# Dealing the MLP units of a decode kernel to partitions in runs of 4, with b1 loaded as rows

## The chip, the cores and the metric

The kernel runs on one core of one Trainium2 chip. The time is device microseconds (us) of one execution, lower is better. A median is over the runs of one kernel. A trace is one profiled execution; its times count from the start of the span.

## The reference, cut to what matters

```python
h  = x + attention(layernorm(x), k_cache, v_cache, wq, wo)   # 4 x 32 heads x 4096 keys x 128, bf16
hn = layernorm(h)                                            # 4 rows of 640
u  = hn @ w1 + b1                                            # w1: 640 x 1728
a  = u * tanh(softplus(u))                                   # mish
h2 = h + a @ w2                                              # w2: 1728 x 640
```

The caches are 268 MB and are read once. The MLP is small, but it comes last. Its 1728 hidden units may be dealt to the 128 partitions in any order, as long as the columns of w1, the elements of b1 and the rows of w2 are dealt alike.

## The kernel before: the parts that matter

Five engine programs run side by side. One queue (issued by SP) loads in this order: wq, all K and V tiles, wo, w1 in three pieces (2, 2 and 1 of the 5 row groups), w2 in four. The small loads go through ACT's queue. 1728 = 13 * 128 + 64, so there are 13 full groups of 128 units and a rest of 64.

```python
W1S = (0, 2, DC - 1, DC)          # pieces of w1
W2S = (0, 6, 10, 12, FM)          # pieces of w2: 6+4+2+1 of 13 row groups (FM = 13)

# b1: partition p holds units 13p .. 13p+12, runs of 26 B; the rest of 64 units 2 B each
load(ac, b1T[:, 0:FM], B_b1[0 : FM * P].rearrange("(p j) -> p j", j=FM), "b1a", "S")
load(ac, b1T[0:FT, FM : FM + 1], B_b1[FM * P : F].rearrange("(p o) -> p o", o=1), "b1b", "S")

# w2: the same dealing, 13 rows running for each partition
w2_v = B_w2[0 : FM * P, :].rearrange("(p j) n -> p j n", j=FM)
for k, (j0, j1) in enumerate(zip(W2S, W2S[1:])):
    load(sp, w2_sb[:, j0:j1, :], w2_v[:, j0:j1, :], ("w2", j0), ...)

# TensorE: w1 is the stationary operand; group j is every 13th column
for c0, c1 in zip(W1S, W1S[1:]):
    # ... before the last piece: two matmuls add b1_hi and b1_lo ...
    pe.need(("w1", c0))
    for j in [FM] + list(range(FM)):
        for c in range(c0, c1):
            if j < FM:
                w = w1_sb[:, c, 0 : FM * P].rearrange("p (f j) -> p j f", j=FM)[:, j, :]
            else:
                w = w1_sb[:, c, FM * P : F]
            mm(h1_ps[...], w, cen[:, c, :], ...)
# ... then DVE and ACT: h1, exp, mish -> act; TensorE: 4 matmuls for each row group of w2 ...
for j0, j1 in zip(W2S, W2S[1:]):
    pe.need(("w2", j0))
    for j in range(j0, j1):
        w2_mm(j)
```

The softmax here doesn't subtract the row's maximum and nothing guards it: scores larger than these inputs give would overflow.

## Time and profile before

| | before |
|---|---|
| median of 3 runs | 662.52 us (662.31 to 663.42) |
| span of the profiled run | 661.0 us |
| read from HBM | 283.35 MB, 429 GB/s over the span |
| busy: DVE, PE | 62%, 58% |

The page of the kernel before has one row of the DMA engines' busy tenths, in 40 slices of 16.5 us, and the page gives the rate over the span:

```profile
DMA  9999999999999999999999999999999999999997
HBM read 283.35 MB, written 0.01 MB: 429 GB/s over the span
```

DMA is the limit of everything but the end: only the last slice is below nine tenths. What comes behind the last landings is a chain of compute. In order of time, the last pieces of the chain of waits of the kernel before (start us, length us, what):

```profile
628.31 23.43 DMA slotB<-in_B_w_dram
651.73 0.04 issue
651.78 3.07 PE red L714 x44
...
654.87 0.23 DVE h L677
...
656.42 0.23 DVE act L703
656.64 0.04 issue
656.69 2.16 PE red L714 x55
658.85 0.02 issue
658.87 0.33 DVE o_bf L710
```

The second piece of w1 lands at 651.73 us. From there to o_bf at 658.87 us nothing but compute is on the chain. The timeline of the same stretch gives the groups (start us, length us, engine, line, operation, output and inputs, count, and in brackets the idle time before with what ended it; PEld is the weight load):

```profile
651.78 1.83 PEld L714 LDWEIGHTS red<-cen,slotB 128*64 128x64 bf16 x28 [0.21 <-DMA slotB<-in_B_w_dram]
653.74 1.01 PEld L714 LDWEIGHTS red<-cen,slotB 128*64 128x64 bf16 x14
656.69 0.30 PE L714 MATMUL red<-w_tail,act 64*4 64x160 bf16 x4 [1.10 <-DVE act L703]
656.92 1.90 PE L714 MATMUL red<-slotA,act 128*4 128x160 bf16 x52
```

The w1 loads take 1.83 us for 28 and 1.01 us for 14; in steady state one starts every 58 to 61 ns. (A row of the timeline is named by the shape of its first load; of the 28, two have 64 columns and 26 have 128.) The 52 w2 matmuls run in 1.90 us, 36.5 ns each on average, without a wait. The pieces of w2 land at 655.08, 656.67, 657.45 and 657.84 us by the trace, so each has landed when it is reached, but the last less than 1 us ahead.

### The profile page before, as it was taken

What the parts mean: (1) busy time and instruction counts of PE and PEld (TensorE: products, weight loads), DVE (VectorE), ACT (ScalarE), POOL (GpSimd) and SP (SyncE); (2) the same over time, 40 slices, a digit from 0 to 9 for tenths busy, and PEclk for the clock granted to TensorE, in tenths of its full rate; (3) what the DMA queues carried; (4) which work ended last, traced back from release to release, by engine and by line L of the source; (5) the groups of instructions that cost most, each with busy time, mean ns of one, the idle gap of its engine ahead of it and who ended that gap; (6) DMA issues with size and microseconds to landing.
All of it is one profiled execution on the core that took longest, in us unless ns stands there. A gap on an engine that the chain in (4) does not pass through costs nothing. (4 is left out here: it accounts for less than half of the span.)

```text
span 661.0 us, 4948 instructions
## 1 busy us (share of the span) xinstructions
PE 386.6 (58%) x2623; PEld 70.5 (11%) x1663; DVE 407.4 (62%) x255; ACT 40.7 (6%) x157; POOL 1.7 (0%) x12
## 2 busy tenths in 40 slices
PE   0356667457317595838307485828534757675877
PEld 0100010101101010101100010100110001010146
DVE  2067889386049778677219688948306798857612
ACT  0200000000000000000000000000000000000011
POOL 0000000000000000000000000000000000000000
PEclk9998698879659796869668778977965879786865
DMA  9999999999999999999999999999999999999997
GB/s 386 444 440 444 421 408 445 437 441 437 429 420 440 436 436 436 440 428 424 444 432 432 440 428 424 444 432 433 444 436 432 424 440 428 440 440 428 412 418 303
DMA packets 7121, 283.48 MB, mean 429 GB/s; under 512 B 1028, under 2 KB 1352, under 8 KB 2376
## 3 DMA queue, kind: packets, MB, share of 16 engines
q1 hardware_dynamic: 6784, 283.27, 99.2%
q10 hardware_dynamic: 328, 0.09, 0.1%
q8 instruction: 6, 0.10, 0.1%
q14 instruction: 3, 0.02, 0.0%
HBM read 283.35 MB, written 0.01 MB: 429 GB/s over the span
## 5 line engine op out<-in xcount | busy, mean ns | idle before, releaser
L513 DVE TENSOR_TENSOR slotA<-slotA,q_bc 128x8192 bf16<-128x8192 bf16 x32 | 140.6, 4415 | 106.2 <-DMA slotA<-in_A_k_cache_dram 106.2
L513 DVE TENSOR_TENSOR slotB<-slotB,q_bc 128x8192 bf16<-128x8192 bf16 x32 | 140.7, 4416 | 17.6 <-DMA slotB<-in_A_k_cache_dram 17.6
L524 DVE TENSOR_REDUCE s_f<-red 128x64 f32<-128x1024 f32 x64 | 78.0, 1218 | 96.8 <-PE red L724 96.8
L724 PE MATMUL red<-slotA,ident 128*128 128x512 bf16 x480 | 135.3, 445 | 0.0
L724 PE MATMUL red<-slotB,ident 128*128 128x512 bf16 x480 | 127.4, 425 | 0.0
L714 PE MATMUL red<-slotA,ident 128*128 128x512 bf16 x32 | 14.4, 451 | 127.7 <-PEq L49 127.7
L714 PE MATMUL pv<-slotC,e 128*32 128x512 bf16 x768 | 52.9, 436 | 37.4 <-PEq L49 34.4
L714 PE MATMUL red<-slotB,ident 128*128 128x512 bf16 x32 | 14.1, 441 | 88.3 <-PEq L49 88.3
L393 ACT ACTIVATE ex<-s_f 128x64 bf16<-128x64 f32 x64 | 16.4, 256 | 513.3 <-DVE s_f L524 513.3
L538 DVE TENSOR_TENSOR e<-ex,hmask 128x512 bf16<-128x512 bf16 x64 | 39.8, 683 | 0.0
L714 PEld LDWEIGHTS pv<-slotC,e 128*32 128x32 bf16 x768 | 22.6, 107 | 94.3 <-issue 80.7
L714 PEld LDWEIGHTS red<-slotA,ident 128*128 128x128 bf16 x32 | 3.2, 99 | 195.7 <-issue 195.7
L714 PEld LDWEIGHTS red<-slotB,ident 128*128 128x128 bf16 x32 | 3.2, 99 | 172.1 <-issue 172.1
L714 PEld LDWEIGHTS o_ps<-pv_sb,selo 128*32 128x32 f32 x136 | 13.5, 109 | 64.5 <-issue 64.5
L714 PE MATMUL o_ps<-pv_sb,selo 128*32 128x128 f32 x136 | 18.0, 276 | 0.0
L714 PE MATMUL pv<-slotA,e 128*32 128x512 bf16 x256 | 14.5, 380 | 0.3 <-PEq L49 0.3
L403 ACT COPY pv_sb<-pv 128x512 f32<-128x512 f32 x16 | 9.4, 585 | 68.6 <-PE pv L714 68.6
L393 ACT ACTIVATION_READ_ACCUMULATOR ex<-s_f 128x1 f32 x64 | 11.9, 186 | 0.0
L714 PEld LDWEIGHTS pv<-slotA,e 128*32 128x32 bf16 x256 | 6.7, 97 | 23.4 <-issue 17.5
L563 DVE RECIPROCAL rl<-misc 32x1 f32<-32x1 f32 x4 | 0.6, 150 | 12.7 <-PE misc L714 12.7
L714 PE MATMUL red<-slotC,lnT 128*32 128x512 bf16 x40 | 4.5, 629 | 6.7 <-PEq L49 6.7
L714 PE MATMUL y_ps<-a_t,slotB 128*128 128x4 bf16 x160 | 7.0, 179 | 0.2
(99 smaller groups left out, 67.2 us busy)
## 6 DMA issues: line engine op xcount, KB each, us to landing
slotC<-in_A_v_cache_dram SPq DMA_DIRECT2D x2, 4096.0 KB, 39.3
slotC<-in_A_wq_dram SPq DMA_DIRECT2D x1, 5120.0 KB, 16.4
slotB<-in_A_wo_dram SPq DMA_DIRECT2D x3, 1280.0 KB, 15.9
slotB<-in_B_w_dram SPq DMA_DIRECT2D x2, 864.0 KB, 22.6
slotA<-in_B_w_dram SPq DMA_DIRECT2D x1, 960.0 KB, 20.8
slotB<-in_A_wo_dram SPq DMA_DIRECT2D x1, 640.0 KB, 19.6
slotA<-in_B_w_dram SPq DMA_DIRECT2D x1, 640.0 KB, 19.7
slotB<-in_A_wo_dram SPq DMA_DIRECT2D x1, 480.0 KB, 20.3
```

Of the source, the lines that this page charges most:

```text
L393: lambda: a.activation(out=ex[:, sl], in_=s_f[:, sl], func=ACT.Exp, scale=SCALE, accum_out=rs[:, b, s : s + 1],),
L403: lambda: a.copy(out=pv_sb[:, :, :].rearrange("p r d -> p (r d)"), in_=pv[:, :]),
L513: lambda: v.tensor_tensor(out=t, in0=t, in1=q_bc[:, hg, b, :].unsqueeze(1).to_broadcast([P, RS, Dh]), op=ALU.mult,),
L524: lambda: v.tensor_reduce(out=s_f[:, s * RS : (s + 1) * RS], in_=red[:, k : k + 2, :].rearrange("p k (r c) -> p (k r) c", c=CW), axis=AX.X ...
L538: lambda: v.tensor_tensor(out=e[:, sl, :], in0=ex[:, sl].unsqueeze(2).to_broadcast([P, RS, G]), in1=hmask[:, :].unsqueeze(1).to_broadcast( ...
L563: dv.do(lambda: v.reciprocal(out=rl[:, :], in_=l_ps), ("rl", hg), DV)
L714: lambda: nc.tensor.matmul(out_, lhsT=lhsT, rhs=rhs, start=start, stop=stop, skip_group_check=skip),
L724: return t.add_instruction(mybir.InstMatmult(name=nc.get_next_instruction_name(), engine=mybir.EngineType.PE, ins=[t.lower_ap(rhs), t.lowe ...
```

## The change

The intent: a run of 4 units for each partition, so that the columns of w1 for one group lie 4 elements (8 B) apart and not 13 (26 B); with it w2 falls into contiguous blocks of 512 rows; and b1 comes in as three rows of 512 and one of 192 units, which TensorE turns into columns, in place of 192 runs of 26 B and 2 B.

```diff
+    FI = 4
+    FB = FM // FI
+    F0 = FB * FI * P
 ...
-    W2S = (0, 6, 10, 12, FM)
+    W2S = tuple(range(0, FM, FI)) + (FM,)
 ...
-        w2_v = B_w2[0 : FM * P, :].rearrange("(p j) n -> p j n", j=FM)
 ...
-            load(sp, w2_sb[:, j0:j1, :], w2_v[:, j0:j1, :], ("w2", j0), ...)
+            load(
+                sp, w2_sb[:, j0:j1, :],
+                B_w2[j0 * P : j1 * P, :].rearrange("(p j) n -> p j n", j=j1 - j0), ("w2", j0), ...)
 ...
-        ac.need("b1z")
-        load(ac, b1T[:, 0:FM], B_b1[0 : FM * P].rearrange("(p j) -> p j", j=FM), "b1a", "S")
-        load(ac, b1T[0:FT, FM : FM + 1], B_b1[FM * P : F].rearrange("(p o) -> p o", o=1), "b1b", "S")
+        load(ac, b1r[:, :], B_b1[0:F0].rearrange("(k f) -> k f", k=FB), "b1a", "B0")
+        load(ac, b1e[:, :], B_b1[F0:F].rearrange("(o f) -> o f", o=1), "b1b", "B1")
 ...
+        dv.need("b1p", "b1z")
+        dv.do(lambda: v.tensor_copy(out=b1T[:, 0:FM], in_=b1_ps[:, 0:FM]), "b1m", DV)
+        dv.do(lambda: v.tensor_copy(out=b1T[0:FT, FM:FC], in_=b1_ps[0:FT, FM:FC]), "b1T", DVP)
 ...
+        pe.need("b1a", "b1b")
+        for k in range(FI):
+            mm(b1_ps[:, k : FB * FI : FI],
+               b1r[:, :].rearrange("k (f i) -> k i f", i=FI)[:, k, :], ident[0:FB, 0:FB], True, True)
+        mm(b1_ps[:, FM - 1 : FM], b1e[:, 0:P], ident[0:1, 0:1], True, True)
+        mm(b1_ps[0:FT, FM:FC], b1e[:, P : P + FT], ident[0:1, 0:1], True, True, "b1p")
 ...
-                    if j < FM:
-                        w = w1_sb[:, c, 0 : FM * P].rearrange("p (f j) -> p j f", j=FM)[:, j, :]
+                    if j < FB * FI:
+                        k, i = divmod(j, FI)
+                        w = w1_sb[:, c, k * FI * P : (k + 1) * FI * P]
+                        w = w.rearrange("p (f i) -> p i f", i=FI)[:, i, :]
                     else:
-                        w = w1_sb[:, c, FM * P : F]
+                        w = w1_sb[:, c, j * P : min((j + 1) * P, F)]
```

The rows of b1 lie in the space of the first V tile until they are turned, so the first V load now waits for the turn.

More of the change, by code (lines that the diff above doesn't have):

```diff
@@ L122 @@
     WSEM = ["WQ", "WT"] + [f"W{k}" for k in range(13)]
-    for s in ["PE", "DV", "DVP", "DVA", "AC", "ACP", "PO", "KA", "KB", "VA", "VC", "V2", "X", "S", "OUT0", "OUT1", "FIN"] + WSEM:
+    for s in ["PE", "DV", "DVP", "DVA", "AC", "ACP", "PO", "KA", "KB", "VA", "VC", "V2", "X", "B0", "B1", "OUT0", "OUT1", "FIN"] + WSEM:
         book.handles[s] = nc.alloc_semaphore(s)
@@ L173 @@
     wq = slot["C"][:, 0 : DC * H * Dh].rearrange("p (c n) -> p c n", c=DC)
+    b1r = sb("b1r", (FB, FI * P), BF16, setup, topC)
+    b1e = sb("b1e", (1, F - F0), BF16, setup, topC)
     x_bf = sb("x_bf", (N, D), BF16, setup, topC)
@@ L226 @@
     l_ps = misc[0:BG, 64:65]
+    b1_ps = pv[:, 0:FC]
     a_ps = misc[:, 128 : 128 + G * N].rearrange("p (j n) -> p j n", n=N)
@@ L246 @@
     dv = Prog(nc.vector, book)
-    pe = Prog(nc.tensor, book, take=["DVP", "DVA", "ACP", "VA", "VC", "V2"] + WSEM)
+    pe = Prog(nc.tensor, book, take=["DVP", "DVA", "ACP", "VA", "VC", "V2"] + WSEM + ["B0", "B1"])
     def tiles(src, i):
@@ L307, in sync_prog @@
                 k_load(i + 1)
-            sp.need(("PV", i - 1) if hg else ("qb", N - 1))
+            sp.need(("PV", i - 1) if hg else "b1p")
             v_load(i)
@@ L330, in sync_prog @@
         sp.need(("PV", NT - 2))
-        w2_v = B_w2[0 : FM * P, :].rearrange("(p j) n -> p j n", j=FM)
         for k, (j0, j1) in enumerate(zip(W2S, W2S[1:])):
-            load(sp, w2_sb[:, j0:j1, :], w2_v[:, j0:j1, :], ("w2", j0), f"W{len(WOS) + len(W1S) - 1 + k}")
+            load(
+                sp, w2_sb[:, j0:j1, :],
+                B_w2[j0 * P : j1 * P, :].rearrange("(p j) n -> p j n", j=j1 - j0), ("w2", j0),
+                f"W{len(WOS) + len(W1S) - 1 + k}",
+            )
         store(sp, 0)
@@ L649, in dve_prog @@
         dv.do(lambda: v.tensor_copy(out=h_hi[:, :, :], in_=st[:, :, :]), "h_hi", DV)
-        dv.need("std2", "b1b")
+        dv.need("std2")
         dv.do(
@@ L768, in pe_setup @@
             )
+        pe.need("b1a", "b1b")
+        for k in range(FI):
+            mm(
+                b1_ps[:, k : FB * FI : FI], b1r[:, :].rearrange("k (f i) -> k i f", i=FI)[:, k, :],
+                ident[0:FB, 0:FB], True, True,
+            )
+        mm(b1_ps[:, FM - 1 : FM], b1e[:, 0:P], ident[0:1, 0:1], True, True)
+        mm(b1_ps[0:FT, FM:FC], b1e[:, P : P + FT], ident[0:1, 0:1], True, True, "b1p")
     def fold(i, s):
@@ L926, in pe_prog @@
         pe_setup()
-        pe.need("selo", "xT")
+        pe.need("selo", "xT", "b1T")
         logs = []
```

## The prediction

> **What bounds it now.** DMA. The page shows the 16 DMA engines at nine tenths or more in 39 of 40 slices, 429 GB/s over a 661.0 us span; DVE is 62% busy, PE 58%. Loads leave one queue in order, so only behind the last loads does compute count. The chain of waits ends: w1 transfer until 651.73; 44 weight load and matmul pairs until 654.85; h1, exp and mish 1.8 us; at 656.69 the 56 w2 matmuls until 658.85; o_bf; stores. The trace's landings: w1 second piece 651.73, third 652.80; w2 655.08, 656.67, 657.45, 657.84. The w2 matmuls pass their pieces without a wait, so the end is compute behind w1, with w2 less than 1 us behind it.
>
> **What the change touches.**
> 1. *w1 weight loads at stride 4 (8 B) in place of 13 (26 B).* In the timeline the stride-13 pairs follow each other every 59 to 61 ns; the wo pairs, same shape at stride 5 (10 B), every 40 ns, at the same granted clock of 0.50. [...] Stride 4 should reach about 40 ns. Behind 651.73 stand 42 w1 pairs, 39 of which gain 20 ns: about 0.8 us. The third piece would still come in time (the second would be done at about 653.0).
> 2. *w2 pieces of 4+4+4+1 rows.* Same bytes. By packet times in the trace (7680 B 291 ns, 5120 B 196, 2560 B 102, 1280 B 57) the engine time is 82.7 us before, 82.6 after: neutral. But the piece before the last grows from 2 rows to 4, so 5 rows (20 matmuls at 36.5 ns) stand behind 657.45, not 3. With act ready at about 655.9, rows 8 to 11 would be awaited for about 0.2 us. So of 0.8 us about 0.6 remain.
> 3. *b1 as rows.* It removes 252 packets of 2 to 26 B, each recorded at 9 ns: 0.1 us of DMA time at most. b1's landing (42.2 us before) moves to about 17 to 21 us. It adds 6 small matmuls (about 0.3 us) on PE at about 23.6 us and two DVE copies of about 0.15 us. The first cache multiply waits for K until 35.87, so they are hidden. The first V load is issued about 0.5 us later than 23.62, but the queue holds K data until about 54 us: no loss.
>
> **Sum.** About 0.6 us at the tail and 0.1 us of DMA: **661.8 us** from 662.52, range **661.0 to 662.7**. Chances: faster by over 2% 0.01, within 2% 0.98, slower by over 2% 0.01.
>
> **What would show each step.**
> - 1: w1 pairs at about 40 ns in the timeline; from the second piece's landing to h1 about 2.3 us, not 3.1.
> - 2: w2's last landing, relative to w1's, within 0.3 us of before; a new wait of PE for w2 of 0.1 to 0.4 us within the last 20 matmuls.
> - 3: no packets under 100 B of b1; b1T ready before 30 us; the first multiply still released by K at about 36 us; no new gap before the first V.
>
> **What would make it wrong.** The landings differ by up to 2 us between the 16 DMA engines; if the new order shifts which is last, the end moves by some tenths either way, as much as the gain. If stride 4 loads no faster, the gain is 0.1. If b1's rows land after about 35 us, the first multiply starts late; there, too, the queue holds over 15 us of work. If w1 then waits for its third piece, part of 1 is lost.

The step to "about 40 ns" rests on the wo loads, measured at 40 ns. 0.6 us at the tail and 0.1 us of DMA off 662.52 us come to 661.8 us.

## The result

The changed kernel measured 662.26 us, median of 4 runs (661.73 to 662.73), beside 662.41 us of the kernel before in the same rounds (662.31 to 663.42). The ratio is 0.9994, interval 0.9977 to 1.0011: the same within 2%, and not clear of noise by this measurement alone. Repeated twice it was 0.9986, just clear of 1 (interval 0.9973 to 0.9999), and 0.9991, not clear (below). The profiled span is 660.5 us and not 661.0.

The chain of waits of the changed kernel ends so:

```profile
639.61 17.80 DMA slotA<-in_B_w_dram
657.41 0.04 issue
657.46 0.86 PE red L725 x20
658.32 0.02 issue
658.35 0.33 DVE o_bf L721
```

The chain before hung on w1 (slotB); now it hangs on w2 (slotA), and only 20 matmuls stand behind the landing. The timeline of the changed kernel, for the groups shown of the kernel before:

```profile
651.75 1.11 PEld L725 LDWEIGHTS red<-cen,slotB 128*64 128x64 bf16 x28 [0.89 <-DMA slotB<-in_B_w_dram]
653.00 0.65 PEld L725 LDWEIGHTS red<-cen,slotB 128*64 128x64 bf16 x14
655.59 0.30 PE L725 MATMUL red<-w_tail,act 64*4 64x160 bf16 x4 [1.10 <-DVE act L714]
655.82 1.24 PE L725 MATMUL red<-slotA,act 128*4 128x160 bf16 x32
657.46 0.84 PE L725 MATMUL red<-slotA,act 128*4 128x160 bf16 x20 [0.40 <-DMA slotA<-in_B_w_dram]
```

The w1 loads fell from 1.83 to 1.11 us and from 1.01 to 0.65 us. The activation is used at 655.59 and not at 656.69 us. Then TensorE, which never waited here before, stands still for 0.40 us (its weight loads for 0.74 us) until the third piece of w2 has landed.

To compare traces whose bulk loads are some tenths apart, one interval serves below, called the tail: from the first w1 weight load that the second piece's landing releases, to the start of o_bf. It splits at the first w2 matmul:

| | first part: w1, b1, mish | second part: w2 | tail |
|---|---|---|---|
| before | 656.69 - 651.78 = 4.91 | 658.87 - 656.69 = 2.18 | 7.09 |
| changed | 655.59 - 651.75 = 3.84 | 658.35 - 655.59 = 2.76 | 6.60 |

So 1.07 us were gained in the first part, and 0.58 us of them given back in the second: 0.49 us in all, which is the difference of the spans (0.5 us). The landings did not move: w1's second piece came at 651.73 before and 651.71 us after, w2's last at 657.84 and 657.83 us.

At the start of the changed kernel, the turning of b1 looks like this in the timeline:

```profile
22.05 0.29 PE L725 MATMUL pv<-ident,b1r 3*128 3x3 bf16 x4
22.20 0.27 PE L725 MATMUL pv<-ident,b1e 1*128 1x1 bf16 x2
22.50 0.33 SPq L260 DMA_DIRECT2D slotC<-in_A_v_cache_dram  x1
22.51 0.17 DVE L514 CAST b1T<-pv 128x13 bf16<-128x13 f32 x1 [13.00 <-PE pv L725]
...
35.31 8.76 DVE L524 TENSOR_TENSOR slotA<-slotA,q_bc 128x8192 bf16<-128x8192 bf16 x2 [12.54 <-DMA slotA<-in_A_k_cache_dram]
```

It is over 12 us before the first K tile lands and releases the first multiply. The rows landed at 15.7 and 20.4 us; nothing waited for them.

### The profile page after: what moved, and what is told of

It is laid out like the page before. It is cut to its first block, busy times and chain, and to the rows that moved or that the text cites. A ratio compares the mean times of both kernels' runs of the same rounds, so it can differ in the third digit from the quotient of the medians.

```text
span 660.5 us, 4963 instructions
## 1 busy us (share of the span) xinstructions
PE 390.8 (59%) x2628; PEld 69.1 (10%) x1669; DVE 407.9 (62%) x257; ACT 40.7 (6%) x157; POOL 1.7 (0%) x12
## 5 line engine op out<-in xcount | busy, mean ns | idle before, releaser
L735 PE MATMUL red<-slotA,ident 128*128 128x512 bf16 x480 | 138.8, 453 | 0.0
L735 PE MATMUL red<-slotB,ident 128*128 128x512 bf16 x480 | 130.3, 432 | 0.0
L725 PE MATMUL red<-slotA,ident 128*128 128x512 bf16 x32 | 14.3, 446 | 127.7 <-PEq L49 127.7
L725 PE MATMUL red<-slotB,ident 128*128 128x512 bf16 x32 | 14.1, 440 | 85.6 <-PEq L49 85.6
```

The source lines that it names most:

```text
L725: lambda: nc.tensor.matmul(out_, lhsT=lhsT, rhs=rhs, start=start, stop=stop, skip_group_check=skip),
L735: return t.add_instruction(mybir.InstMatmult(name=nc.get_next_instruction_name(), engine=mybir.EngineType.PE, ins=[t.lower_ap(rhs), t.lowe ...
```

## The experiments

The theory (A): the byte stride of the w1 weight loads sets how fast they follow each other; this shortens the first part by 1.1 us, and then the landing of w2's four-row piece, which did not move, gives more than half back. The rivals: (B) the gain is chance in the order of landings; (C) the end is set by the landing of w2's last piece alone; (D) the new pieces of w2 did it; (E) b1's small packets did it (E2, in the later runs: each tiny packet costs the bulk loads some time); and (G) to (J), other laws for the stride, against F, whose numbers follow the slope from 32 ns at 8 B to 40 ns at 10 B. In the expectations, a pair is a weight load with its matmul.

All kernels of this section gave correct results.

### The changed kernel again: after_again and after_third

No edit.

> The changed kernel again, as the yardstick of this group. Theory A (stride of the w1 weight loads shortens the compute behind w1 by 1.1 us; w2's four-row piece, whose landing did not move, gives 0.6 us of it back): time 0.3 to 0.6 us under before, so a ratio of 0.9992 to 0.9996, possibly not clear of noise. Rival B (the tail is shorter by chance of the landing order): the ratio scatters about 1.000, and the profile's w2 landing differs from the 657.4 us of the first profile.

> The changed kernel a third time, as yardstick of this group. So far it measured 0.9994 and 0.9986 of the time before; theory A puts 0.5 us (0.9992) at the tail. If rows of b1 save DMA time as well (theory E2), 0.5 to 0.9 us in all, 0.9986 to 0.9992.

Measured: 661.48 us, median of 5 (661.36 to 661.87), beside 662.42 us before, ratio 0.9986 (0.9973 to 0.9999); and 662.11 us, median of 5 (661.35 to 662.62), beside 662.36 us, ratio 0.9991 (0.9977 to 1.0004). The tail was 658.35 - 651.75 = 6.60 us and 658.00 - 651.40 = 6.60 us, the same as in the first profile to 0.01 us, although w1's and w2's landings in the third trace were 0.35 us earlier. So the gain at the tail is no chance, and rival B falls. The scatter of the times is as large as the gain. Nearly all of those 0.35 us can be put down to one load: the 4 MB load of V near 461 us landed 19.96 and 19.91 us after the load before it in the first two traces and 19.63 in the third, where most such steps are 19.3 us; the load before it had landed at 441.5 to 441.6 us in all three. Why this load varies is not known.

### w2_pieces_only

```diff
 # on the kernel before
-    W2S = (0, 6, 10, 12, FM)
+    W2S = (0, 4, 8, 12, FM)
```

> The kernel before with w2 in pieces of 4+4+4+1 rows, still 13 rows apart, w1 at stride 13. Theory A: the activation is ready only near 656.7 us, groups 8 to 11 are reached near 657.9, after their landing near 657.4: no wait, no change, ratio 1.000 and o_bf near 658.9. Rival D (the pieces themselves help or harm, whatever w1 does): o_bf moves by 0.2 us or more.

Measured: 662.22 us, median of 5 (661.93 to 662.47), ratio 0.9997 (0.9984 to 1.0010). The tail was 658.56 - 651.49 = 7.07 us (7.09 before), and the 52 w2 matmuls ran in 1.90 us without a wait. D falls for the pieces alone. (This kernel leaves the rows 13 apart; the contiguous blocks are tested only together with the stride.)

### b1_row_only

On the kernel before: b1 as one row of 1728 units, turned by 14 matmuls, each reading every 13th unit; the dealing, w1 and w2 as before.

```diff
-        load(ac, b1T[:, 0:FM], B_b1[0 : FM * P].rearrange("(p j) -> p j", j=FM), "b1a", "S")
-        load(ac, b1T[0:FT, FM : FM + 1], B_b1[FM * P : F].rearrange("(p o) -> p o", o=1), "b1b", "S")
+        load(ac, b1r[:, :], B_b1.rearrange("(o f) -> o f", o=1), "b1a", "B0")
 ...
+        for j in range(FM):
+            row = b1r[:, 0 : FM * P].rearrange("o (f i) -> o i f", i=FM)[:, j, :]
+            mm(b1_ps[:, j : j + 1], row, ident[0:1, 0:1], True, True)
+        mm(b1_ps[0:FT, FM:FC], b1r[:, FM * P : F], ident[0:1, 0:1], True, True, "b1p")
```

> The kernel before with b1 alone loaded as one row and turned by 14 matmuls; w1 stays at stride 13, w2 in its pieces of 6+4+2+1. Theory A: w1 pairs stay at 59 to 61 ns, o_bf stays near 658.9 us, DMA landings move by under 0.1 us, ratio 1.000. Rival E (the tiny packets of b1 cost DMA time or shift which engine is last, and that is the gain): landings and o_bf come about 0.5 us earlier, ratio near 0.9993.

Measured: 662.23 us, median of 6 (661.86 to 670.65). One run took 670.65 us; it makes the ratio 1.0022 (0.9983 to 1.0060). No trace of that run exists, and it stays unexplained; the other five have a mean of 662.16 us. The tail was 658.68 - 651.55 = 7.13 us, that of the kernel before. So b1 does nothing for the tail. Whether its rows save the bulk loads some 0.1 us, as predicted, this run can't tell: w1's second piece landed at 651.51 and not 651.73 us, within the 0.35 us by which repeats of one kernel differ.

### b1_small_runs and b1_small_again

On the changed kernel: the dealing in runs of 4 kept, b1 loaded straight into place, 3 * 128 runs of 8 B and 192 of 2 B, no turn.

```diff
-        load(ac, b1r[:, :], B_b1[0:F0].rearrange("(k f) -> k f", k=FB), "b1a", "B0")
-        load(ac, b1e[:, :], B_b1[F0:F].rearrange("(o f) -> o f", o=1), "b1b", "B1")
+        for k in range(FB):
+            load(ac, b1T[:, k * FI : (k + 1) * FI],
+                 B_b1[k * FI * P : (k + 1) * FI * P].rearrange("(p i) -> p i", i=FI), ("b1", k), "S")
+        load(ac, b1T[:, FM - 1 : FM], B_b1[F0 : F0 + P].rearrange("(p o) -> p o", o=1), "b1a", "S")
+        load(ac, b1T[0:FT, FM:FC], B_b1[F0 + P : F].rearrange("(p o) -> p o", o=1), "b1b", "S")
 # the six matmuls and the two copies that turn b1 are left out
```

> The changed kernel with b1 loaded straight into place, as 384 packets of 8 B and 192 of 2 B, no TensorE turn. Theory A: w1 pairs at 32 ns, o_bf near 658.35 us as in the changed kernel; b1 lands much later than 42 us (estimate from 9.4 us for each 4 packets per engine beside the bulk queue: 36 packets per engine, 80 to 90 us), which nobody waits for; ratio 0.999 to 1.000. Rival E (b1's packets matter): o_bf comes back to near 658.9 us or later.

> The changed kernel with b1 in 576 packets of 8 B and 2 B again. Theory E2 (each tiny packet costs the DMA stream time, by its recorded 9 ns at least: 656 packets with the semaphore writes, 0.37 us over 16 engines): 0.3 to 0.7 us over after_third; the bulk landings fall behind before 100 us and stay behind. Theory A alone (b1 packets cost nothing): equal to after_third within 0.15 us.

Measured: 662.34 us, median of 4 (662.28 to 662.52), ratio 0.9997 (0.9981 to 1.0014); and 662.39 us, median of 5 (662.28 to 663.01), ratio 1.0001 (0.9987 to 1.0014), beside 662.11 us of the changed kernel on the same chip. The tail was 658.71 - 652.13 = 6.58 us and 658.73 - 652.15 = 6.58 us: the gain at the tail is there without the rows. But the bulk came later: w1's second piece landed at 652.09 and 652.11 us, while in the three traces of the changed kernel it landed at 651.71, 651.71 and 651.36. That is 0.5 us on average (652.10 - 651.59), about the 0.3 to 0.7 us expected, and it eats the gain of the tail. Expectation A alone (o_bf near 658.35 us; within 0.15 us of the changed kernel) failed here: o_bf came at 658.71 and 658.73 us. So E2 holds for b1 in this form: with the dealing in runs of 4, b1 has to come some other way than in 576 tiny packets, and the rows do that. (The two landings lie 0.36 us above the latest of the eleven other traces, b1_elements left out (651.36 to 651.73), so part of the 0.5 us may be scatter.) The kernel before had 192, a third of them; its cost is within the scatter: 651.73 us, and 651.44 in w2_pieces_only, which has the same 192.

These traces also show the pace of tiny packets beside the bulk queue. The last of b1 landed at 101.2 us in the first of them; 576 packets over 16 engines are 36 for each, which from about 14 us on are one in 2.4 us, and a 64 KB packet of the bulk queue is recorded at 2.42 us. The trace of the kernel before has the same pace: between 17.07 and 28.01 us its packets of 26 B start in five groups of 16, 2.42 us from group to group. So about one tiny packet per engine started in the time of one bulk packet. What makes it so was not shown.

### b1_elements

On b1_small_runs: the 12 dealt groups in 12 loads of 128 single elements, so 1728 packets of 2 B in 14 loads.

```diff
-        for k in range(FB):
-            load(ac, b1T[:, k * FI : (k + 1) * FI], ...)
+        for j in range(FB * FI):
+            k, i = divmod(j, FI)
+            src = B_b1[k * FI * P : (k + 1) * FI * P].rearrange("(p i) -> p i", i=FI)[:, i : i + 1]
+            ac.do(lambda: ac.eng.dma_start(out=b1T[:, j : j + 1], in_=src,
+                                           allow_slow_non_contiguous=True), ("b1", j), "S", 16)
```

> The changed kernel with b1 as 1728 packets of 2 B in 14 loads, three times as many packets as the small runs. Theory E2: 1952 packets with the semaphore writes, 1.1 us over 16 engines by the recorded 9 ns, up to 2 us; so 1 to 2 us over after_third, late bulk landings up to some 250 us. Theory A alone: within 0.2 us of after_third.

Measured: 688.53 us, median of 5 (685.93 to 690.08), ratio 1.039 (1.0369 to 1.0412): 26 us over the kernel before, where E2 expected 1 to 2 us and A under 0.2. The timeline of this kernel shows why:

```profile
3.42 50.40 ACTq L369 DMA_DIRECT2D b1T<-in_B_b_dram  x12
53.84 1.76 ACTq L257 DMA_DIRECT2D b1T<-in_B_b_dram  x2
55.63 1.28 ACT L378 ACT_TABLE_LOAD   x1 [55.63 <-issue]
56.93 0.29 ACT L378 ACTIVATE std<-mv,eps 4x1 f32<-4x1 f32 x1
...
64.55 0.33 SPq L257 DMA_DIRECT2D slotC<-in_A_v_cache_dram  x1
```

ACT issues these loads in its own instruction stream, and the issue of 12 of them took 50.4 us. They were not alike: the first eight took about 0.4 to 0.5 us each, the next four 7.3, 17.9, 18.6 and 2.7 us. So an issue has no fixed cost here; what held the later ones was not tested. The layernorm's square root stands behind them on ACT and came at 56.93 and not at 6.79 us as in the kernel before; with it q, the first V load (64.55 and not 23.62 us), and the first K multiply (66.00 us). The bulk queue ran dry. The DMA view of this kernel for the window of 0 to 120 us (3 us each slice) has it:

```profile
DMA  7999988899889988971009798899000988998898
```

The second gap (from about 84 to 93 us) is the K load that waits for the late multiplies. Against b1_small_again, the fifth bulk load landed 22.7 us later (116.92 and 94.18 us) and w1's second piece 24.0 us later (676.06 and 652.11 us); the tail itself was the changed kernel's (682.78 - 676.10 = 6.68 us). So this run does not measure what a tiny packet costs the stream. It shows instead that a load's issue can hold up the engine that issues it (here up to 18.6 us for one load).

### The law of the stride: stride_16B, stride_12B, stride_24B, stride_4B

On the changed kernel: other runs of units, with b1 as one row (turned by 14 matmuls, each reading its units at the same stride as w1), and w2's pieces fitted to the blocks (4+4+4+1; for 12 B 4+2+2+4+1; for 4 B six of 2 and one of 1).

```diff
-    FI = 4
+    BLK = ((0, 8), (8, 4), (12, 1))     # stride_16B; (first group, run) of each block
+    BLK = ((0, 6), (6, 6), (12, 1))     # stride_12B
+    BLK = ((0, 12), (12, 1))            # stride_24B
+    BLK = ((0, 2), (2, 2), ... (10, 2), (12, 1))   # stride_4B
 ...
+                        b0, n = block(j)
+                        w = w1_sb[:, c, b0 * P : (b0 + n) * P].rearrange("p (f i) -> p i f", i=n)[:, j - b0, :]
```

The figures that stand at the cuts are F's. They come from spacings measured before: 32 ns at 8 B and 40 ns at 10 B are 4 ns for each byte of stride, so 48 ns at 12 B and 64 ns at 16 B; the 60 ns at 26 B says that the growth ends somewhere, and that it ends at 16 B was the assumption. At 4 B, F expected the 26 to 28 ns of contiguous loads.

> Units dealt in runs of 8, then 4, then 1, so w1 read at strides of 16 B (8 groups), 8 B (4) and 2 B (1); w2 pieces 4+4+4+1. [...] 64 ns or at least the 60 ns of 26 B. Rival G (cost grows with the byte distance): about 45 to 50 ns, between 10 B and 26 B.

> Units dealt in runs of 6, 6 and 1: w1 read at stride 12 B. [...] 48 ns. Rival G (grows slowly with the distance up to 60 ns at 26 B): about 42 ns. Rival H (only two speeds, fast to 8 B and slow beyond): 60 ns, but then the 40 ns at 10 B would be odd.

> Units dealt in runs of 12 and 1: w1 read at stride 24 B. [...] 60 to 64 ns. Rival G (distance): about 57 ns. Rival I (alignment: a stride that is a multiple of 8 B is kinder than 26 B): clearly under 55 ns.

> Units dealt in runs of 2: w1 read at stride 4 B, w2 in six pieces of two rows and one of one. [...] at 8 B the pitch was 32 ns, contiguous loads 26 to 28 ns; [...] should sit at the floor, 26 to 28 ns. Rival J (32 ns at 8 B is already the floor of any strided load): 32 ns. End set by the w2 landing either way, o_bf 0.4 us after it.

Each ran once, so the state of the run is unknown; they are read within their traces alone, for the spacing of the weight loads (32 ns in all three traces of the changed kernel) and for the tail, and not for their times. The w1 weight loads behind the second landing, in the timelines of 16 B (mixed: 8 groups at 16 B, 4 at 8 B), 12 B, 24 B and 4 B, one kernel in each fence:

```profile
651.45 1.57 PEld L731 LDWEIGHTS red<-cen,slotB 128*64 128x64 bf16 x28 [0.48 <-DMA slotB<-in_B_w_dram]
```
```profile
651.52 1.45 PEld L731 LDWEIGHTS red<-cen,slotB 128*64 128x64 bf16 x28 [0.59 <-DMA slotB<-in_B_w_dram]
```
```profile
651.61 1.73 PEld L731 LDWEIGHTS red<-cen,slotB 128*64 128x64 bf16 x28 [0.31 <-DMA slotB<-in_B_w_dram]
```
```profile
651.68 0.97 PEld L731 LDWEIGHTS red<-cen,slotB 128*64 128x64 bf16 x28 [1.04 <-DMA slotB<-in_B_w_dram]
```

From the starts of the single loads in the same traces, in steady state (medians behind the second landing; for wo, of all its loads). The last column is a second witness, from the same kernels and b1_row_only: the loads that turn b1 between 21.9 and 23.9 us, one partition of 128 columns at the stride of the dealing (the granted clock was 1.00 in the changed kernel from 22.0 to 22.4 us):

| stride | kernel | ns from load to load | ns per byte of stride | turn of b1, ns |
|---|---|---|---|---|
| 4 B | stride_4B | 27 | 6.8 | 27 |
| 8 B | changed | 32 | 4.0 | 32 (stride_16B) |
| 10 B | wo, in before | 40 | 4.0 | |
| 12 B | stride_12B | 47 | 3.9 | 47 |
| 16 B | stride_16B | 61 | 3.8 | 60 |
| 24 B | stride_24B | 58 | 2.4 | 59 |
| 26 B | before | 59 | 2.3 | 60 (b1_row_only) |

From 8 B to 16 B the spacing is 3.8 to 4.0 ns for each byte of stride (32 to 61 ns), and from 16 B on it grows no further (61, 58 and 59 ns). A law by distance (G) would put 16 B between 10 and 26 B, and it came out as the slowest; two speeds only (H) is contradicted by 40 and 47 ns; a bonus for multiples of 8 B (I) by 58 ns at 24 B (61 ns behind the third landing). 27 ns at 4 B is off this slope, which would give 16 ns, and it is below the 32 ns at 8 B, so J falls too. The granted clock was 0.50 in the stretches behind the second landing (asked for before, the changed kernel, b1_row_only, 16 B, 12 B and 24 B); the wo loads took 40 ns in a stretch at 0.96 as well (before, 641.7 to 643.4 us), and the turn of b1, at 1.00 in the changed kernel, gives the same series. What the traces fix is how the spacing hangs on the stride; why it does is not shown.

The four kernels show the pinning as well. The tails:

| kernel | tail, us |
|---|---|
| before, 59 ns | 7.09 |
| stride_24B, 58 ns | 658.58 - 651.61 = 6.97 |
| stride_16B, 61 and 32 ns mixed | 658.15 - 651.45 = 6.70 |
| stride_12B, 47 ns | 658.16 - 651.52 = 6.64 |
| changed, 32 ns | 6.60 |
| stride_4B, 27 ns | 658.29 - 651.68 = 6.61 |

Below 47 ns faster weight loads gave nothing: the landing of w2 is what comes last. At 47 ns the first part was 0.49 us longer than in the changed kernel (4.33 and 3.84 us), and this cost only 0.04 us at the end. stride_24B is the control for the stride: it has b1 as a row and the w2 pieces 4+4+4+1, and with 58 ns it keeps most of the tail of the kernel before (6.97 of 7.09 us). But stride_12B and stride_4B have w2 in other pieces, so their ends do not depend on the weight loads alone.

### fine_w2_end

On the changed kernel, the four-row piece before the last in two halves.

```diff
-    W2S = tuple(range(0, FM, FI)) + (FM,)
+    W2S = (0, 4, 8, 10, 12, 13)
 ...
-                B_w2[j0 * P : j1 * P, :].rearrange("(p j) n -> p j n", j=j1 - j0), ("w2", j0),
+                w2_block(j0, j1), ("w2", j0),     # rows of the block of 4, cut to j0..j1
```

> The changed kernel with w2 row groups 8 to 11 loaded as two pieces of two, so pieces of 4+4+2+2+1. Theory A: groups 8 and 9 land about 0.8 us earlier (near 656.6 us), their 8 matmuls run before the landing of 10 and 11 (near 657.4), 12 matmuls of 36.5 ns stand behind that or 4 behind the last (657.83); o_bf starts near 658.05 us and not 658.35, so 0.3 us less than the changed kernel, ratio to before near 0.9988. Rival C (the end is set by the landing of the last piece alone, or finer pieces cost DMA time): o_bf does not move, or later landings eat it.

Measured: 661.47 us, median of 5 (661.39 to 661.60), ratio 0.9986 (0.9973 to 0.9999), beside 661.48 us of the changed kernel on the same chip. In its timeline:

```profile
655.50 1.51 PE L732 MATMUL red<-slotA,act 128*4 128x160 bf16 x40
657.21 0.69 PE L732 MATMUL red<-slotA,act 128*4 128x160 bf16 x12 [0.20 <-DMA slotA<-in_B_w_dram]
657.60 0.09 PEld L732 LDWEIGHTS red<-slotA,act 128*4 128x4 bf16 x4 [0.29 <-DMA slotA<-in_B_w_dram]
657.96 0.32 DVE L728 CAST o_bf<-red 128x160 bf16<-128x160 f32 x1 [2.74 <-PE red L732]
```

Now 40 matmuls run before the wait and not 32, and even the very last four wait for their piece, which landed at 657.56 us. But o_bf started 0.40 us after that landing, and in the changed kernel 0.52 us (658.35 - 657.83). The tail is 657.96 - 651.46 = 6.50 us: 0.10 us gained and not 0.3. I had counted the last four matmuls at their spacing, 0.15 us, and left out that o_bf starts about 0.35 us after the last one does (657.61 to 657.96 us; a w2 matmul is recorded at 329 ns on average here, with its end modelled). So C is nearly right for what is left: the last piece's landing plus 0.40 us is the least seen, here and in stride_4B (657.89 to 658.29 us), whose pieces are finer still, and the changed kernel is 0.12 us above it. In time, no difference from the changed kernel shows. It beats the kernel before by the same 0.14%, and is the fastest measured, by nothing that can be told from noise.

## Why the prediction was right, point by point

The time fell into the range (662.26 us; 661.0 to 662.7), and the direction, the size at the tail (0.6 us predicted, 0.49 us in the traces) and "within 2%" were right. The range is no proof of the mechanism: the kernel before, at 662.41 us, lies in it too. What speaks for the mechanism is the tail. By step:

1. *The w1 loads at stride 4 (8 B) would follow each other every 40 ns, 0.8 us off the chain.* The mechanism held; the size was low: 32 ns, and the first part of the tail shrank by 1.07 us. The mis-sized term is the spacing. I took the wo loads at 10 B as the floor, and they were a point on the slope: 10 B against 8 B, 40 ns against 32. The third piece of w1 did come in time (landed at 652.77 us, needed at 653.00).
2. *w2's landings would not move, a new wait of about 0.2 us would take back a quarter.* The landings held (w1's second to w2's last: 6.11 us before, 6.12 after). The wait came where it was predicted, before the last 20 matmuls. TensorE is recorded idle for 0.40 us, since the matmul before it still runs; by the starts, 0.74 us passed where 0.13 is usual, so 0.6 us, and this is the 0.58 us given back. It was larger than the predicted 0.2 us mainly because the activation was there at 655.59 and not at about 655.9 us, as step 1 gained more and ran against the same landing; the other 0.1 us is that four w2 matmuls start every 134 ns, 33.5 each and not 36.5. So the errors of steps 1 and 2 cancel for the most part, and that the sum came within about 0.1 us is due to the landing that caps it and not to the sizes. That is why a wrong spacing did little harm to the time, and stride_12B shows it as an experiment, since even 47 ns give nearly the same tail.
3. *b1 hidden at the start, 0.1 us of DMA time at most.* Hidden, yes: landed at 15.7 and 20.4 us (predicted 17 to 21), the first multiply released by K at 35.31 us, no gap before the first V. That V load was issued at 22.50 us, not 0.5 us later than the 23.62 us before, so this guess was wrong in sign; nothing hung on it. The number of packets was miscounted: of the 252, 60 were packets of 4 B that are no data of b1, and 32 such remain; the queue of the small loads went from 328 packets to 112. The 0.1 us can neither be shown nor denied: the landings at the end agree to 0.02 us in the first pair of traces, but this is chance: at 441.5 us the changed kernel was 0.26 us ahead, and lost most of it in the one load that varies. Repeats differ by 0.35 us at the end, and at the 441 us mark kernels with rows lie between 441.48 and 441.86 us, the two with 192 direct packets at 441.74 and 441.78. What b1's rows do is avoid what the new dealing would have cost with direct loads, 0.5 us by the two runs of small packets.
4. *What would make it wrong.* The 2 us between the engines are in the trace of the kernel before: the 16 landings of one load lie 1.9 to 2.0 us apart for all of w1 and w2. The scatter of the landings, named there, is what the single measurements show: 0.9994, 0.9986 and 0.9991 for the same kernel with the same tail.

The change gains little for a plain reason. The whole MLP tail that it touches is 7 us of 661; the w1 loads are 3 us of it; and w2's landing stood less than 1 us behind.

## What to carry to other kernels

Where weights are read with a stride, choose the dealing so that the stride is small; here the spacing of 128-column loads fell from 59 ns at 26 B to 32 ns at 8 B, and to 27 ns at 4 B, while 16 B gained nothing (61 ns). Before making a chain behind one landing shorter, look up how far behind the next landing is: that distance is the most that can be gained (here 1.07 us were gained in the first part and 0.58 us given back in the second), and after that the size of the piece behind the last landing counts (0.52 us from the last landing to o_bf here, 0.40 with finer pieces). Load a bias vector as rows and turn it on TensorE if the alternative is hundreds of tiny runs (here 576, with landings 0.5 us later, part of which may be scatter), and keep such loads out of the instruction stream of an engine that has to compute soon (b1_elements lost 26 us to this).
